# A second hand-written order for the steps of an interleaved convolution loop

## The chip, the cores and the metric

One Trainium2 chip, one of its cores. The metric is the device time of one launch in microseconds (us), the median of several runs. Engines are named as in the profile: PE (TensorE, matmuls), DVE (VectorE), ACT (ScalarE), POOL (GpSimd), SP (the queue that issues most DMAs). In this kernel POOL's instructions read and write SBUF alone; those of DVE and ACT also read PSUM.

## What is computed

A block with two halves. The first normalizes x (2048 x 640), modulates it, and applies a state-space convolution along the 2048 positions; the second is a gated feed-forward layer. What matters here is the first half, above all its kernel K:

```python
dt = jnp.exp(log_dt)[:, None]
logdA = dt * (A_re + 1j * A_im)                # 640 channels x 128 states
P = jnp.exp(logdA[:, :, None] * l)             # l = 0 .. 2047
K = jnp.einsum("dn,dnl,dn->dl", Cc, P, dt * Bc).real
y = irfft(rfft(u, 2 * L) * rfft(K, 2 * L))[:, :L] + u * Dskip
x = x + ga * y                                 # u is the normalized, modulated x
h = layernorm(x) * (1 + cb) + sb
x = x + gb * ((silu(h @ w1) * (h @ w3)) @ w2)
```

## The kernel before

The kernel runs in three stretches: tables, modulation and a first transform of x (to about 168 us), the convolution (to about 420 us), and the feed-forward layer (the rest, bound by PE's matmuls). The change lies in the convolution.

The 640 channels are cut into NS = 40 steps of SD = 16 channels. For each step k, two pipelines of named parts are run, one that makes the kernel's transform for the 16 channels, one that multiplies and inverts transforms made earlier (its index runs ten ahead of its own first block: its step k works on the block (k - 10) // 8 of 128 channels, part (k - 10) % 8).

Making the kernel, step k:

- `PH` (`phases`, POOL): two integer instructions, L469 over 1024 and L470 over 512 elements, give the angles `ph`. There are four `ph` buffers: PH of k waits until both readers on DVE of k - 4, `A1` and `A2`, are through.
- `AB`, `CO`, `SI` (`absph`, `cosine`, `sine`, ACT): the absolute value, then cosine and sine of the angles, into `cs` (three buffers) and back into `ph`.
- `PA`, `XA`, `PQ`, `XQ` (`exp_fast`, `fast`, `exp_slow`, `slow`): two small matmuls on PE into a PSUM tile, ACT's exponential out of it into the table `A`; then the same with another matmul pair. All four use one PSUM buffer, tag "B", so that they run strictly one after the other over all steps.
- `E1`, `E2`, `A1`, `A2` (`real1`, `real2`, `imag1`, `imag2`, DVE; L494, L497, L501, L505): products of `A` with cosine and sine. Both inputs and the output are in SBUF.
- `kg` (`kgen`, PE, L518): 64 small matmuls into the PSUM tile `pk` (one buffer).
- `K` (`k1evac`, DVE, L525 and L526): reads `pk` from PSUM.
- `pt` (`k_stage1`, PE, L536), `uk` (`k_out`, ACT): first stage of the transform of K.

The convolution, step k:

- `st` (`stage2`, PE, L567): second stage of both transforms into the PSUM tile `p` (one buffer: st of k waits for Y of k - 1).
- `kc` (`k_copy`, ACT): half of `p` to SBUF.
- `T` (`products`, DVE, L584 and L585) and `Y` (`sums`, DVE, L591 and L592): the complex product; each of these four instructions has one input in PSUM.
- `iv` (`inverse1`, PE, L609) into the PSUM tile `pz` (one buffer for two steps), `zt` (`z_store`, ACT and DMA): the inverse transform out to DRAM.

Loads (`s2` in stage2, `i1` in inverse1, `uk` from DRAM in `u_load`) and the stores of `zt` are issued on SP.

The order in which these parts stand on each engine is written out by hand in the list `ROUND` (L823). It is a list of words such as `XA+4`; round `rnd` runs `XA` of step 4 * rnd + 4, and skips what is out of range or already done. One round holds four steps of each part (two stores `zt`). `in_order[0] = True` before the loop makes `keep` hold every engine's instructions in the order in which the list names them. The steps up to about 10 are done before the loop, in another order, and the last of the convolution (from step 42 on) after it. Instructions of different engines are tied only by their data and buffers; the list sets no order between engines.

ACT has to load a table when it goes between the exponentials (`XA`, `XQ`) and the cosine and sine.

## Time and profile before

| what | us |
|---|---|
| median of 3 runs | 987.19 |
| the runs | 982.88, 987.19, 990.32 |
| the profiled execution | 988.51 |
| its span in the trace | 986.7 |

The trace is that of the profiled execution. Its times start at the span's start. In the trace the convolution's first `T` starts at 168.69 us and its last at 415.35; `PH` of the last step starts at 351.24 us. Lines with an "x" and a count are groups; durations are in ns in views by tile or by line and in us in the timeline. A bracket at the end of a timeline row gives the idle time of that engine ahead of the instruction and what the profile holds to have ended it. "PEclk" is the clock granted to PE as a share of the full one.

### The profile page before, as it was taken

How to read it: one execution, taken by the hardware profiler on the slowest of the kernel's cores; microseconds unless marked ns; L12 is line 12 of the kernel's file. 1: busy time of each engine (PE TensorE's matmuls, PEld its weight loads, DVE VectorE, ACT ScalarE, POOL GpSimd, SP SyncE). 2: the span in 40 equal slices, each digit the busy share in tenths (PEclk: the TensorE clock that was granted, in tenths of full speed). 3: DMA queues.
4: the chain of work that ended last, by engine and by line, in shares of the span. 5: the costliest groups of instructions: out<-in, count | busy, mean ns of one | idle time of the engine just before them, and what ended most of it. 6: DMA issues, size and time to landing. Idle time of an engine off the chain costs nothing.

```text
span 986.7 us, 20165 instructions
## 1 busy us (share of the span) xinstructions
PE 897.5 (91%) x7984; PEld 675.2 (68%) x7984; DVE 719.0 (73%) x1259; ACT 545.4 (55%) x797; POOL 275.3 (28%) x278
## 2 busy tenths in 40 slices
PE   4896787888788889889999999999999999999998
PEld 2443444666666666567788888777888888888886
DVE  5598876999999997667766665568796766654575
ACT  4568675989999884246533332355653333323432
POOL 1473233455454550213522220112152222200000
PEclk8657787999999999989999999999999999999999
DMA  9462576544655477767211311897422221112443
GB/s 264 154 239 103 204 195 195 154 124 142 169 156 145 147 210 217 246 179 250 81 45 59 107 57 54 213 270 225 135 93 67 81 67 54 54 41 87 153 147 121
DMA packets 103570, 140.72 MB, mean 143 GB/s; under 512 B 20564, under 2 KB 62676, under 8 KB 103476
## 3 DMA queue, kind: packets, MB, share of 16 engines
q1 hardware_dynamic: 99668, 129.34, 43.9%
q0 software_dynamic: 2304, 7.74, 2.3%
q10 hardware_dynamic: 1504, 2.36, 0.8%
q8 instruction: 63, 1.03, 0.4%
q14 instruction: 31, 0.25, 0.1%
HBM read 107.94 MB, written 31.46 MB: 141 GB/s over the span
## 4 chain that ended last, share of the span: by engine, by line
PE 67%; DVE 17%; ACT 7%; DMA 4%; issue 3%; SPq 1%; POOL 0%; ACTq 0%; DVEq 0%; POOLq 0%
PE ps L102 54%; DVE E L494 3%; DVE E L497 3%; PE p L567 2%; PE pk L518 2%; DMA zs<-zt 2%; PE pz L609 2%; ACT cs L135 1%; PE pt L536 1%; DVE p L585 1%; DVE A L501 1%; ACT ph L135 1%; DVE T L584 1%; DVE A L505 1%; PE pu L408 1%
## 5 line engine op out<-in xcount | busy, mean ns | idle before, releaser
L102 DVE TENSOR_TENSOR s<-ps,s 128x512 f32<-128x512 f32 x138 | 94.9, 688 | 79.9 <-PE ps L102 79.6
L469 POOL TENSOR_TENSOR ph<-thi,iota 128x1024 int32<-128x1024 int32 x40 | 85.5, 2137 | 166.2 <-DVE pk L525 61.6
L102 DVE TENSOR_TENSOR gl<-rw,gh 128x640 fp32r<-128x640 f32 x87 | 78.2, 899 | 67.5 <-ACT gh L102 67.4
L102 ACT CAST gh<-rw 128x640 fp32r<-128x640 f32 x87 | 63.3, 727 | 106.3 <-PE ps L102 62.5
L567 PE MATMUL p<-uk,s 128*64 128x256 f32 x640 | 79.7, 391 | 14.5 <-issue 9.0
L102 PE MATMUL ps<-xA,gh 128*128 128x512 f32 x280 | 87.9, 392 | 0.4 <-ACT xA L102 0.4
L102 PE MATMUL ps<-gh,uh 128*128 128x512 f32 x224 | 87.4, 390 | 0.0
L102 PE MATMUL ps<-gl,uh 128*128 128x512 f32 x224 | 87.2, 389 | 0.0
L102 POOL TENSOR_TENSOR S<-rw 128x256 f32<-128x256 f32 x46 | 36.7, 800 | 173.9 <-DVE S0l L102 154.8
L102 PE MATMUL ps<-gh,ul 128*128 128x512 f32 x208 | 81.1, 390 | 0.0
L567 PEld LDWEIGHTS p<-uk,s 128*64 128x64 f32 x640 | 46.2, 140 | 38.6 <-issue 14.1
L102 PEld LDWEIGHTS ps<-xA,gh 128*128 128x128 f32 x280 | 52.1, 188 | 13.0 <-ACT xA L102 1.0
L494 DVE TENSOR_TENSOR E<-A,cs 128x1024 f32<-128x1024 f32 x40 | 56.1, 1402 | 5.9 <-ACT cs L135 5.2
L518 PE MATMUL pk<-E 128*32 128x64 f32 x1280 | 46.5, 235 | 14.1 <-DVE K L526 14.0
L102 PE MATMUL ps<-xA,gl 128*128 128x512 f32 x140 | 54.5, 390 | 0.0
L518 PEld LDWEIGHTS pk<-E 128*32 128x32 f32 x1280 | 32.9, 117 | 30.5 <-DVE K L526 17.3
L470 POOL TENSOR_TENSOR ph<-ph,phi 128x512 int32<-128x512 int32 x40 | 51.7, 1292 | 4.0 <-DVE phi L293 1.0
L536 PE MATMUL pt<-s,K 128*64 128x128 f32 x640 | 49.1, 295 | 1.8 <-ACT uk L138 1.8
L609 PE MATMUL pz<-Y,i 64*128 64x128 f32 x640 | 46.1, 285 | 4.0 <-ACT zt L138 3.7
L501 DVE TENSOR_TENSOR A<-A,ph 128x1024 f32<-128x1024 f32 x40 | 49.1, 1227 | 0.0
L609 PEld LDWEIGHTS pz<-Y,i 64*128 64x128 f32 x640 | 40.3, 191 | 12.3 <-issue 6.0
L102 ACT ACTIVATE s<-ps 128x512 f32<-128x512 f32 (+1 forms) x33 | 19.7, 597 | 51.5 <-PE ps L102 51.5
(255 smaller groups left out, 2291.8 us busy)
## 6 DMA issues: line engine op xcount, KB each, us to landing
rw<-in_w_dram SPq DMA_DIRECT2D x52, 320.0 KB
us<-u SPq DMA_DIRECT2D x16, 640.0 KB
s<-in_s_dram SPq DMA_DIRECT2D x40, 256.0 KB
i<-in_i_dram SPq DMA_DIRECT2D x40, 256.0 KB
rw<-in_wg_dram SPq DMA_DIRECT2D x31, 320.0 KB
rw<-in_wu_dram SPq DMA_DIRECT2D x28, 320.0 KB
uk<-us SPq DMA_DIRECT2D x32, 256.0 KB
zs<-zt SPq DMA_DIRECT2D x32, 256.0 KB
```

The costliest lines, as they stand in the source:

```text
L102: ins = fn(*args, **kw)
L135: return tc.keep_in_program_order(S.activation(*args, **kw))
L408: PE.matmul(pu[h][hh * 64:hh * 64 + 64, q, :320], s1r[r], x[r, hh * 320:hh * 320 + 320], start=not (one and h == 0), stop=True, tile_posit ...
L469: hold(G.tensor_tensor(p, bc(thi[:, sl], 2, NPH), bc(iota, 1, SD), op=OP.mult))
L470: keep(G.tensor_tensor(p[:, :, :NA], p[:, :, :NA], bc(phi[:, sl], 2, NA), op=OP.add))
L494: keep(V.tensor_tensor(EC[s][:, :, 1:3, :], AA[s][:, :, 1:3, :], mid(cs[s]), op=OP.mult))
L497: keep(V.tensor_tensor(EC[s][:, :, 0, :], AA[s][:, :, 0, :], cs[s][:, :, 2 * NA - 1:NA - 1:-1], op=OP.mult))
L501: keep(V.tensor_tensor(A[:, :, 1:3, :], A[:, :, 1:3, :], mid(ph[s]), op=OP.mult))
L518: keep(PE.matmul(pk[dq * 32:dq * 32 + 32, g, :], x[:, g * 4 + dq, 1, :], x[:, g * 4 + dq, 0:3:2, :], start=(st == 0), stop=(st == 1), tile ...
L536: keep(PE.matmul(pt[c * 64:c * 64 + 64, g, :], kk[:, g, :], s1[:, c, :], start=True, stop=True, tile_position=(0, c * 64)))
L567: keep(PE.matmul(p2[par * 64:par * 64 + 64, pi, c, :], s2[:, pi * 2 + par, c * 64:c * 64 + 64], uk[:, 0:kn + 1:kn, f, :], start=True, stop ...
L609: ins = keep(PE.matmul(pz[:, par, (g % 2) * 2 + pi, :], i1[r, pi, c, :], Y[r, pi, c, :], start=(c == 0), stop=(c == 1), tile_position=(par ...
```

## The change

Only the list `ROUND` is replaced. Both lists hold the same 22 parts, `zt` for two steps and each other part for four, so the work of a round is the same; what differs is the order, and how far apart the steps of different parts stand. No instruction, buffer or DMA is added or taken away.

```diff
     ROUND = (
-        "A1+0 pt-2 K-1 st+1 CO+1 E1+1 iv-1 uk-2 pt-1 kc+1 zt-1 kg+0 PH+4 T+1 CO+2 uk-1 E2+1 Y+1 SI+1 E1+2 "
-        "st+2 A2+1 K+0 AB+4 SI+2 E2+2 SI+4 CO+3 A1+1 kc+2 A2+2 CO+4 PA+4 iv+0 pt+0 SI+3 kg+1 T+2 iv+1 Y+2 "
-        "E1+3 XA+4 A1+2 st+3 PQ+4 kc+3 XQ+4 PA+5 uk+0 K+1 XA+5 zt+1 kg+2 T+3 PQ+5 PH+5 XQ+5 pt+1 PA+6 Y+3 "
-        "AB+5 XA+6 E2+3 st+4 PH+6 AB+6 A1+3 PQ+6 A2+3 XQ+6 kc+4 iv+2 uk+1 PA+7 E1+4 E2+4 PH+7 K+2 XA+7 T+4 "
-        "kg+3 AB+7 A2+4 PQ+7 Y+4 XQ+7 "
+        "XA+6 PQ+6 pt+2 A2+3 AB+6 XQ+6 kc+4 A1+4 PH+7 T+4 uk+2 PA+7 iv+2 Y+4 kg+3 K+3 XA+7 CO+5 A2+4 PQ+7 "
+        "st+5 AB+7 kg+4 kc+5 E1+5 T+5 CO+6 iv+3 SI+7 SI+5 K+4 Y+5 pt+3 PH+8 uk+3 E2+5 E1+6 A2+5 A1+5 st+6 "
+        "zt+3 AB+8 E2+6 SI+6 kc+6 iv+4 CO+7 T+6 CO+8 iv+5 kg+5 SI+8 XQ+7 pt+4 Y+6 K+5 st+7 PA+8 PH+9 uk+4 "
+        "A2+6 XA+8 PQ+8 kc+7 XQ+8 A1+6 E1+7 kg+6 PH+10 AB+9 T+7 PA+9 pt+5 Y+7 K+6 XA+9 E1+8 uk+5 PQ+9 E2+7 "
+        "XQ+9 E2+8 zt+5 A1+7 PA+10 st+8 "
     ).split()
     in_order[0] = True
     for rnd in range(NS // EB + 3):
```

On DVE a round reads before: A1 K E1 T E2 Y E1 A2 K E2 A1 A2 T Y E1 A1 K T Y E2 A1 A2 E1 E2 K T A2 Y. It reads after: A2 A1 T Y K A2 E1 T K Y E2 E1 A2 A1 E2 T Y K A2 A1 E1 T Y K E1 E2 E2 A1.

## The prediction, on record before the changed kernel ran

> **What bounds the kernel now.** The change touches only the convolution, so I went first to the busy time by windows, cut where the product `T` of every fourth step begins; between 182.50 and 355.00 lie six rounds (first, second and last two rows of the seven; the last is the drain behind the final `PH`).

> ```profile
> core 0: us, PE busy (x) PEld busy (x) DVE busy (x) ACT busy (x) POOL busy (x), PEclk, DMA share, GB/s
> 182.50:211.10 28.60, 23.41 (x472) 17.55 (x472) 27.73 (x41) 26.51 (x33) 14.15 (x9) 1.00 0.55 153
> 211.10:240.00 28.90, 24.81 (x472) 18.93 (x472) 26.28 (x41) 26.47 (x32) 14.36 (x9) 0.94 0.48 135
> ...
> 326.00:355.00 29.00, 24.85 (x472) 18.55 (x472) 27.19 (x42) 26.57 (x32) 16.69 (x13) 0.94 0.57 159
> 355.00:384.00 29.00, 26.29 (x578) 20.47 (x580) 25.94 (x47) 16.85 (x23) 5.26 (x9) 1.00 0.67 190
> ```

> A round lasts (355.0 - 182.5) / 6 = 28.75 us. DVE is busy for up to 27.73 of it, ACT for 26.5, PE for 23.4: DVE is first, but ACT is only 1.2 us behind. That sets how far the time can fall. Next, by tile, the durations of the instructions concerned (min/median/max):

> ```profile
> L469 POOL TENSOR_TENSOR ph<-thi,iota x40: 1892/1906/2819, 15.7 to 351.2; 128x1024 int32<-128x1024 int32 x40
> L470 POOL TENSOR_TENSOR ph<-ph,phi x40: 1042/1047/2109, 18.6 to 354.1; 128x512 int32<-128x512 int32 x40
> L494 DVE TENSOR_TENSOR E<-A,cs x40: 1160/1219/2670, 49.0 to 370.3; 128x1024 f32<-128x1024 f32 x40
> L497 DVE TENSOR_TENSOR E<-A,cs x40: 634/683/2389, 51.1 to 375.3; 128x512 f32<-128x512 f32 x40
> L501 DVE TENSOR_TENSOR A<-A,ph x40: 1209/1218/1494, 53.6 to 375.9; 128x1024 f32<-128x1024 f32 x40
> L505 DVE SCALAR_TENSOR_TENSOR A<-ph,A x40: 677/683/693, 55.2 to 377.0; 128x512 f32<-128x512 f32 x40
> L584 DVE TENSOR_TENSOR T<-p,kc x40: 676/681/693, 168.7 to 415.3; 128x512 f32<-128x512 f32 x40
> L585 DVE TENSOR_TENSOR p<-p,kc x40: 699/699/700, 169.4 to 416.1; 128x512 f32<-128x512 f32 x40
> L591 DVE TENSOR_TENSOR Y<-T,p x40: 411/420/422, 170.2 to 416.8; 128x256 f32<-128x256 f32 x40
> L592 DVE TENSOR_TENSOR Y<-T,p x40: 412/415/421, 170.5 to 417.1; 128x256 f32<-128x256 f32 x40
> L525 DVE TENSOR_TENSOR pk<-pk,dz x40: 155/163/171, 70.3 to 380.3; 128x4 f32<-128x4 f32 x40
> L526 DVE TENSOR_TENSOR K<-pk,gaT x40: 401/424/427, 71.1 to 380.5; 128x256 f32<-128x256 f32 x40
> ```

> The six DVE instructions that read PSUM never stray by more than 26 ns from their least, whatever else runs. E1 and E2, all in SBUF, sometimes take 2.2 and 3.5 times their median, and so do the two of PH. The timeline shows why (rows of other instructions left out):

> ```profile
> 259.33 1.90 POOL L469 TENSOR_TENSOR ph<-thi,iota 128x1024 int32<-128x1024 int32 x1 [2.36 <-DVE pk L525]
> 259.65 0.68 DVE L584 TENSOR_TENSOR T<-p,kc 128x512 f32<-128x512 f32 x1
> 260.05 1.02 ACT L135 ACTIVATE A<-pa 128x1024 f32<-128x1024 f32 x1
> 260.36 0.70 DVE L585 TENSOR_TENSOR p<-p,kc 128x512 f32<-128x512 f32 x1
> 261.31 1.05 POOL L470 TENSOR_TENSOR ph<-ph,phi 128x512 int32<-128x512 int32 x1
> ...
> 261.86 0.61 ACT L135 ACTIVATE A<-pq 128x512 f32<-128x512 f32 x1
> ...
> 263.97 0.68 DVE L505 SCALAR_TENSOR_TENSOR A<-ph,A 128x512 f32<-128x512 f32 x1
> ...
> 264.57 1.21 DVE L494 TENSOR_TENSOR E<-A,cs 128x1024 f32<-128x1024 f32 x1
> 264.79 2.75 POOL L469 TENSOR_TENSOR ph<-thi,iota 128x1024 int32<-128x1024 int32 x1 [2.43 <-DVE A L505]
> 265.71 2.39 DVE L497 TENSOR_TENSOR E<-A,cs 128x512 f32<-128x512 f32 x1
> 267.62 1.37 POOL L470 TENSOR_TENSOR ph<-ph,phi 128x512 int32<-128x512 int32 x1
> ```

> At 259.33 PH runs beside T, and both take their medians. At 264.79 PH starts 0.14 us after A2's end, but E1 has begun; PH's first part ends at 267.54, that is, it ran its 1.9 us only from E1's end on, and E2, issued at 265.71, stood still meanwhile. So a PH instruction and a DVE instruction with both inputs in SBUF exclude each other, whole instructions at a time, and the first to start holds. What that costs is read from the groups in 195 to 350 us:

> ```profile
> L494 DVE TENSOR_TENSOR E<-A,cs 128x1024 f32<-128x1024 f32 x21 | 30.3, 1445 | 3.9 <-ACT cs L135 3.9
> L497 DVE TENSOR_TENSOR E<-A,cs 128x512 f32<-128x512 f32 x21 | 25.6, 1221 | 0.0
> ```

> 21 x ((1.445 - 1.219) + (1.221 - 0.683)) = 16.0 us in 21 steps, 0.76 a step, 3.05 us a round of DVE standing still. The chain of waits runs through it (in order of time: start, us, what):

> ```profile
> 264.65 1.14 DVE E L494
> 265.79 2.31 DVE E L497
> 268.69 1.30 PE pk L518 x64
> ```

> **The change, part by part.** Nothing is added or removed, so the sum is one of waits.

> *DVE.* PH of a step starts when its buffer is free, after A1 and A2 of four steps back. In the new list behind the later of the two stands, each time, one more SBUF instruction (A1+4, E1+5, E2+6, E1+7) and then the run T, Y, K. If that SBUF instruction starts first, PH waits for it and then runs 1.906 + 1.047 and a gap of 0.08 (261.31 less 259.33 less 1.90) = 3.03 us beside T, Y, K, whose medians add up to 0.681 + 0.699 + 0.420 + 0.415 + 0.163 + 0.424 = 2.80. The next SBUF instruction waits about 0.3 us (0.23, and some for the overlap of neighbours). Four times 0.3 is 1.2 a round in place of 3.05: 1.85 off DVE, from 27.73 to 25.9. That lets ACT's 26.5 be the bound.

> *ACT and PE.* What becomes late is the chain of the single buffer "B". From an exponential XA to its XQ the rows at 260.05 and 261.86 give 1.81 us. Between XA+8 and XQ+8 the list puts a copy (kc), between XA+9 and XQ+9 another (uk): XA and one copy fill about 1.5 us, so ACT waits about 0.3 twice. Between PA+10 and the following PQ+6 PE has the whole of st+8:

> ```profile
> 263.00 1.95 PE L567 MATMUL p<-uk,s 128*64 128x256 f32 x16
> ```

> XQ then comes about 1.95 + 0.75 after XA (0.75 is PQ to XQ, 1.81 less XA's 1.02 and a hand-over), filled by XA and AB for 2.0: another 0.5 to 0.7. So ACT's new waits are 0.9 to 1.3 us; with its 26.5 busy, of which a few tenths are tails that a follower overlaps, the round is 27.1 to 27.8. I take 27.4: 28.75 - 27.4 = 1.35 saved, in six rounds 8.1 us.

> [...]

> *The start.* While ACT waits for the first `st`, the old list has A2 of step 10 and the sine of step 12 done; the new one names them behind kc of step 10.

> ```profile
> 168.07 0.59 ACT L138 COPY kc<-p 128x512 f32<-128x512 f32 x1 [7.84 <-PE p L567]
> L135 ACT ACTIVATE ph<-ph x40: 1037/1051/1069, 46.1 to 366.6; 128x1024 f32<-128x1024 int32 x40
> ```

> The cover of 7.84 us is gone for both: on ACT 1.05, on DVE 0.68, at the same time if neither is late otherwise. Between 0 and 1.7, I take 1.0, the larger. *The drain* (355 on) has no PH to exclude, and the two lists end on the same parts: nothing, plus or minus 1. *DMA*: the list sets no order on SP, and where its loads will fall among the stores is not to be read from this trace; nothing is taken for it, with rival (2) as the bound above.

> The sum: 8.1 - 1.0 = 7.1 us off 988.51, 981.4. That execution lies 1.3 above the median of 987.19 and inside 982.88 to 990.32, so beside that median 980, and 981 is taken between the two.

> **The rivals.** (1) *PH gets in first at one E1 a round.* E1+5 needs CO+5, and PH+8 needs A2+4; both hang on the matmul PA+7: CO+5 behind XA and a table load on ACT, A2+4 behind iv and kg on PE and K on DVE.

> ```profile
> 254.83 1.16 PE L609 MATMUL pz<-Y,i 64*128 64x128 f32 x16
> 255.68 1.28 ACT L135 ACT_TABLE_LOAD   x1
> ```
> ```profile
> L135 ACT ACTIVATE cs<-cs,hp x40: 1136/1150/1158, 45.0 to 365.1; 128x1024 f32<-128x1024 f32 x40
> ```
> ```profile
> 297.59 1.10 PE pk L518 x64
> ```

> That is 1.02 + 1.28 + 1.15 = 3.45 for E1 against 1.16 + 1.10 + 0.59 + 0.68 = 3.53, and 0.14 for POOL to start: E1 first, but by 0.2 only. If POOL wins, E1 waits 1.9 us, and T+5, whose kc is ready by then, with it; part of that is swallowed where DVE waits for ACT later in the round. [...] The round is then 28.0 to 28.5: 4.5 to 1.5 saved, less 1.0, for 984 to 987 beside that median. For it: the tie. Against: a DVE that is late for any other reason finds E1's inputs ready and goes first.

> (2) *Slower: PH first at E1+5 and at E1+7 as well.* E1+7 needs XQ+7, which the new list puts behind kc+6, two cosines, a sine and a table load: 2 x 1.15 + 1.05 + 1.28 + 0.61 = 5.24 us, while A1+6, on which PH+10 waits, ends 2.80 + 0.68 + 1.22 = 4.70 behind kc+6 if DVE is not late. If it is less than about 0.4 us late, POOL wins here. DVE then stands 2 x 1.9 more and is spared 0.3 twice: 25.9 + 3.2 = 29.1, plus what it idles now, 28.6 - 27.73 = 0.9: 30.0 a round. That is 1.25 x 6 + 1.0 = 8.5 lost: 996. Against: a loss at one of the two makes DVE late, and so wins the other.

> (3) *All the gain.* ACT's waits vanish behind one another: 26.5, 2.25 x 6 - 1.0 = 12.5 saved, 975. PH and the SBUF instructions, which exclude each other, take 4 x (3.03 + 1.219 + 0.683 + 1.218 + 0.683) = 27.3 by medians, and 26.2 if each of 16 overlaps its follower by the 0.07 us of E1 at 264.57; less is not to be had, and 973 is the floor.

> **How the numbers follow.** Chances: the forecast 0.45, rival (1) 0.20, rival (2) 0.15, rival (3) 0.20. The forecast alone, 27.1 to 27.8 with its start and drain, is 976 to 984; rivals (1) and (3) widen it to 973 and 987, and the drain and the spread of the runs to 990; rival (2) is left out. A difference under 1%, 9.9 us, is taken as none. Faster by more needs 977.3 or less: most of rival (3) and a quarter of the forecast, 0.28. Slower by more needs 997.1: most of what rival (2) holds, with a late load on SP as another way there, 0.15. The rest, 0.57, is neither.

> **What would show it.** Right: the window of a round at 27 to 27.8; the means of E1 and E2 at 1.3 and 0.8 us or less; PH at its medians with T, p, Y and pk beside it; ACT at 95% with waits on PE at XQ. Wrong: rows of E1 over 2 us (rivals 1 and 2), or PE waiting for loads of `s2` and `i1`.

## The result, and the profile after

| what | before | after |
|---|---|---|
| median of 7 runs, us | 983.54 | 975.61 |
| the runs, us | 982.79 to 990.62 | 971.78 to 978.43 |
| the profiled execution, us | 988.51 | 975.61 |
| its span, us | 986.7 | 973.8 |

The ratio of after to before is 0.989, that of the means of the seven runs (985.8 and 975.0 us), with a 95% interval of 0.9854 to 0.9927: 1.1% faster, about 10.8 us, between 7 and 14. The medians lie 7.9 us apart. The forecast was 981 us with "no change over 1%" as the likeliest outcome; the time lies within the range of 973 to 990, and the gain lies above the forecast 7.1. By the means the change is just over 1%, with 1% still inside the interval.

The busy time by windows, cut as before where the product `T` of steps 12, 16, 20 and so on begins (the first two of six rounds, the last, and the drain from T of step 36 to that of 42 and of 49):

```profile
181.13:208.50 27.37, 23.47 (x474) 17.55 (x472) 26.01 (x41) 26.54 (x33) 14.75 (x9) 1.00 0.58 151
208.50:235.87 27.37, 23.47 (x474) 17.55 (x472) 26.03 (x42) 26.52 (x33) 14.75 (x9) 1.00 0.59 155
...
317.98:345.67 27.69, 23.78 (x480) 17.83 (x478) 26.34 (x42) 26.85 (x34) 17.31 (x13) 1.00 0.68 177
...
345.67:378.53 32.86, 30.44 (x624) 23.13 (x624) 26.22 (x49) 20.86 (x30) 8.21 (x11) 1.00 0.86 222
378.53:402.19 23.66, 22.60 (x264) 14.94 (x260) 17.81 (x41) 8.53 (x14) 2.44 (x4) 1.00 0.94 296
```

A round takes 27.37 us, five times within 0.01. ACT is busy for 26.5 of it, 97%, where it was 92%. DVE went from 27.7 to 26.0 busy and is no longer first. No round is granted less than the full PE clock; before, three of six were at 0.94.

The groups of E1 and E2 in 195 to 345 us of the kernel after (count, then busy us in all and mean ns of one, then the idle time before them):

```profile
L494 DVE TENSOR_TENSOR E<-A,cs 128x1024 f32<-128x1024 f32 x22 | 35.2, 1598 | 1.4 <-ACT cs L135 1.4
L497 DVE TENSOR_TENSOR E<-A,cs 128x512 f32<-128x512 f32 x22 | 14.6, 685 | 0.0
```

E2, 1221 ns in the mean before, is at its median: that collision is gone. E1 has become worse, 1598 ns against 1445. The timeline of the kernel after shows one E1 a round that PH gets ahead of:

```profile
238.50 1.15 ACT L135 ACTIVATE cs<-cs,hp 128x1024 f32<-128x1024 f32 x1
238.60 0.79 DVE L505 SCALAR_TENSOR_TENSOR A<-ph,A 128x512 f32<-128x512 f32 x1
239.53 1.90 POOL L469 TENSOR_TENSOR ph<-thi,iota 128x1024 int32<-128x1024 int32 x1 [0.69 <-DVE A L505]
...
239.68 2.84 DVE L494 TENSOR_TENSOR E<-A,cs 128x1024 f32<-128x1024 f32 x1 [0.29 <-ACT cs L135]
...
242.44 0.68 DVE L584 TENSOR_TENSOR T<-p,kc 128x512 f32<-128x512 f32 x1
```

A2+4 ends at 239.39, PH+8 starts 0.14 us later, and the cosine that E1+5 needs ends at 239.65: POOL wins by 0.15 us. E1 then lasts 2.84 instead of 1.22. This is the event of rival (1); its price was not the one given there.

Three traces of each list split the gain: the ones above, the repeats b_ctl and a_ctl, and d_before and d_after, which hold back four loads within the drain and are otherwise the same kernels. Each figure is the difference of two starts of `T`, in us, and the traces stand in that order:

| stretch | old list | new list | means, new less old |
|---|---|---|---|
| T of step 10 to step 12 | 13.84, 13.85, 13.84 | 14.14, 14.15, 14.15 | +0.3 |
| step 12 to 36, six rounds | 172.47, 172.06, 172.05 | 164.54, 164.49, 164.51 | -7.7 |
| step 36 to 49, the drain | 60.35, 59.04, 61.26 | 56.52, 56.63, 57.00 | -3.5 |

They add up to -10.9 us, about the gain of the ratio; without the d pair the drain is -3.1. What lies ahead of step 10 is not touched by the list and moved by itself between 164.7 and 170.0 us; from step 49 to the end of the span it is 571.3 to 571.6 us in all four traces of the two kernels themselves.

### The profile page after: what moved, and what is told of

It reads as the page before. It is cut to its first block, busy times and chain, and to the rows that moved or that the text cites. A ratio compares the mean times of both kernels' runs of the same rounds, so it can differ in the third digit from the quotient of the medians.

```text
span 973.8 us, 20146 instructions
## 1 busy us (share of the span) xinstructions
PE 895.1 (92%) x7984; PEld 672.5 (69%) x7984; DVE 711.6 (73%) x1259; ACT 546.5 (56%) x798; POOL 279.3 (29%) x278
## 3 DMA queue, kind: packets, MB, share of 16 engines
q1 hardware_dynamic: 99668, 129.34, 46.1%
q10 hardware_dynamic: 1504, 2.36, 0.7%
## 4 chain that ended last, share of the span: by engine, by line
PE 76%; ACT 10%; DVE 6%; DMA 4%; issue 3%; POOL 1%; ACTq 0%; SPq 0%; POOLq 0%; DVEq 0%
PE ps L102 55%; PE p L567 6%; ACT A L135 3%; PE pk L518 3%; PE pz L609 3%; PE pt L536 2%; ACT cs L135 2%; DMA zs<-zt 2%; PE pq L441 1%; PE pm L301 1%; PE pa L431 1%; PE pu L408 1%; ACT uk L138 1%; DMA uk<-in_w_mod_dram 1%; ACT L135 1%
## 5 line engine op out<-in xcount | busy, mean ns | idle before, releaser
L469 POOL TENSOR_TENSOR ph<-thi,iota 128x1024 int32<-128x1024 int32 x40 | 91.9, 2297 | 153.9 <-DVE A L501 54.6
L567 PE MATMUL p<-uk,s 128*64 128x256 f32 x640 | 79.4, 390 | 13.9 <-ACT uk L138 5.8
L567 PEld LDWEIGHTS p<-uk,s 128*64 128x64 f32 x640 | 45.9, 139 | 37.8 <-issue 10.1
L494 DVE TENSOR_TENSOR E<-A,cs 128x1024 f32<-128x1024 f32 x40 | 60.4, 1510 | 2.9 <-ACT cs L135 2.2
L470 POOL TENSOR_TENSOR ph<-ph,phi 128x512 int32<-128x512 int32 x40 | 49.5, 1239 | 4.0 <-DVE phi L293 1.0
L501 DVE TENSOR_TENSOR A<-A,ph 128x1024 f32<-128x1024 f32 x40 | 49.9, 1247 | 0.0
L102 PEld LDWEIGHTS ps<-gl,uh 128*128 128x128 f32 x224 | 42.1, 188 | 9.0
L102 PEld LDWEIGHTS ps<-gh,uh 128*128 128x128 f32 x224 | 42.1, 188 | 8.7
L518 PE MATMUL pk<-E 128*32 128x64 f32 x1280 | 46.2, 233 | 1.9 <-issue 1.1
L536 PE MATMUL pt<-s,K 128*64 128x128 f32 x640 | 46.0, 283 | 1.8 <-ACT uk L138 1.8
L609 PE MATMUL pz<-Y,i 64*128 64x128 f32 x640 | 44.5, 283 | 3.0 <-ACT zt L138 2.3
L609 PEld LDWEIGHTS pz<-Y,i 64*128 64x128 f32 x640 | 39.4, 189 | 10.9 <-ACT zt L138 5.2
```

Source lines behind the costliest of these rows:

```text
L102: ins = fn(*args, **kw)
L469: hold(G.tensor_tensor(p, bc(thi[:, sl], 2, NPH), bc(iota, 1, SD), op=OP.mult))
L470: keep(G.tensor_tensor(p[:, :, :NA], p[:, :, :NA], bc(phi[:, sl], 2, NA), op=OP.add))
L494: keep(V.tensor_tensor(EC[s][:, :, 1:3, :], AA[s][:, :, 1:3, :], mid(cs[s]), op=OP.mult))
L501: keep(V.tensor_tensor(A[:, :, 1:3, :], A[:, :, 1:3, :], mid(ph[s]), op=OP.mult))
L518: keep(PE.matmul(pk[dq * 32:dq * 32 + 32, g, :], x[:, g * 4 + dq, 1, :], x[:, g * 4 + dq, 0:3:2, :], start=(st == 0), stop=(st == 1), tile ...
```

## Experiments

**What makes the old round long, and what bounds the new one.** Two kernels cut PH, two cut the cosine. PH of steps 13 on was cut in both lists to one of 16 channels:

```diff
 ...
+        n = SD if s < 13 else 1
-        hold(G.tensor_tensor(p, bc(thi[:, sl], 2, NPH), bc(iota, 1, SD), op=OP.mult))
+        hold(G.tensor_tensor(p[:, :n], bc(thi[:, sl], 2, NPH)[:, :n], bc(iota, 1, SD)[:, :n], op=OP.mult))
 ...
```

The second instruction and the buffer that is kept are left out here.

> The old list, with PH of steps 13 on cut to one of 16 channels (the other angles stay as an earlier step left them), so that POOL hardly occupies SBUF. Exclusion as the cause: E1 and E2 fall to their medians (1.22 and 0.69 us in the mean), DVE loses its 3.05 us of standing still, and the round falls from 28.75 to 26.5 to 27.4 us, where ACT's 26.5 us bind. The rival, that the old order of PE's and ACT's work made the round long and the new list mended that: the round stays at 28.2 us or more.

> The new list with the same small PH. If ACT binds the new round (26.53 us busy of 27.37), it stays at 26.9 to 27.4 us, although the one E1 a round that takes 2.84 us falls to 1.22. If that lost E1 (1.6 us) is on the path, the round falls to 25.8 to 26.3 us.

The old list's windows with the small PH, the first two of six, and then the new list's, first two:

```profile
183.35:209.93 26.58, 23.33 (x478) 17.55 (x477) 24.29 (x41) 26.19 (x33) 3.61 (x8) 1.00 0.61 161
209.93:236.50 26.57, 23.34 (x478) 17.54 (x476) 24.29 (x40) 26.18 (x33) 3.62 (x8) 1.00 0.57 155
```
```profile
180.47:208.64 28.17, 24.89 (x474) 18.72 (x472) 24.55 (x41) 26.29 (x33) 5.74 (x10) 0.94 0.57 145
208.64:235.61 26.97, 23.44 (x474) 17.27 (x474) 24.56 (x40) 26.55 (x33) 4.81 (x7) 1.00 0.60 158
```

E1 and E2 come to 1.22 and 0.71 us in the mean, and the old order falls by 2.0 us a round at full clock (28.53 to 26.57), to 98% ACT. So PH is what made the round long, and the old order of ACT's and PE's work is no worse than the new, rather 0.3 to 0.4 better (26.57 against 26.84 to 26.97 at full clock). The new list loses 0.4 to 0.5 us a round to PH in all, though its E1 stands for 1.6: ACT binds. Two of its six rounds were granted 0.94 and took 28.17, 1.2 us more, which neither expectation allowed for.

One thing this run doesn't separate. A PH that E1 holds up is also late for ACT, which waits for it in every round of the kernel before (182.5 to 355 us: 4.7 in all, 6 times, 1.1 at most):

```profile
ACT cs L135 <- POOL ph L470: 4.7, 6, 1.1
```

The small PH takes away this wait together with DVE's standing still.

The cosine of steps 13 on was cut to half of its channels:

```diff
-        act(cs[s], cs[s], AF.Sin, scale=-2 * math.pi / TURN, bias=hp)
+        c = cs[s] if s < 13 else cs[s][:, :SD // 2]
+        act(c, c, AF.Sin, scale=-2 * math.pi / TURN, bias=hp)
```

> The new list, with the cosine of steps 13 on over half of its channels (the other half keeps the absolute value of the angle), 0.55 us less on ACT a step, 2.2 a round. If ACT binds, the round falls from 27.37 to where DVE stands: 26.0 to 26.4 us. If DVE or PE binds, it stays at 27.2 to 27.4 us.

> The old list, with the cosine of steps 13 on over half of its channels (the other half keeps the absolute value of the angle): 2.2 us less on ACT a round. If DVE, with what it stands still for PH, binds the old round, it stays at 28.2 to 28.8 us, against a fall of 1.5 us that the same cut gave under the new list. If ACT's work binds the old round as well, it falls by 1 us or more.

New list, then old list, two rounds each:

```profile
180.71:206.60 25.89, 23.48 (x474) 17.55 (x472) 24.41 (x42) 24.96 (x33) 14.74 (x9) 1.00 0.62 158
206.60:232.48 25.88, 23.29 (x474) 17.35 (x472) 24.41 (x41) 24.94 (x33) 14.74 (x9) 1.00 0.61 164
```
```profile
212.04:240.57 28.53, 24.76 (x472) 18.82 (x472) 27.50 (x41) 24.87 (x32) 14.15 (x9) 0.94 0.50 141
240.57:269.11 28.54, 23.42 (x472) 17.56 (x472) 28.09 (x42) 24.89 (x32) 14.16 (x9) 1.00 0.55 151
```

With less work on ACT the new round falls by 1.48 us and the old one, at full clock, not at all: ACT's work binds the new round and not the old one, where DVE is busy for 28.09 of 28.54. Less ACT work also settled the tie: E1 came to 1.23 us in the mean under the new list, and DVE no longer waits for its cosine there.

**The ties.** a_swap puts A2+4 behind E1+5 in the new list; a_both also puts A1+6 behind E1+7 (the second pair of lines below is a_both's alone; quotes and line ends of the list are left out).

```diff
-XA+7 CO+5 A2+4 PQ+7 st+5 AB+7 kg+4 kc+5 E1+5 T+5
+XA+7 CO+5 PQ+7 st+5 AB+7 kc+5 E1+5 A2+4 kg+4 T+5
 ...
-PQ+8 kc+7 XQ+8 A1+6 E1+7 kg+6 PH+10 AB+9 T+7 PA+9 pt+5
+PQ+8 kc+7 XQ+8 E1+7 A1+6 PH+10 AB+9 T+7 PA+9 kg+6 pt+5
```

> The new list with A2+4 put behind E1+5 (and kg+4 behind it), so that PH+8 starts only when E1+5 is through. E1 falls from a mean of 1.64 us to 1.22. If E1's lost 1.6 us lies beside an idle DVE and reaches ACT only through the cs buffer that AB+8 waits 0.34 us for, the round falls from 27.37 to 26.9 to 27.2 us, 1 to 3 us off the kernel. If the lost E1 is on the path in full, it falls to 26.0. If K and the matmuls behind the moved kg+4 become late, it rises over 27.5.

E1+5 is spared, and the mean of E1 stays at 1.62 us all the same: DVE now comes earlier to A1+6, and PH+10 gets ahead of E1+7. From the timeline of a_swap:

```profile
237.81 1.23 DVE L494 TENSOR_TENSOR E<-A,cs 128x1024 f32<-128x1024 f32 x1 [0.34 <-ACT cs L135]
...
251.06 0.60 ACT L135 ACTIVATE A<-pq 128x512 f32<-128x512 f32 x1
251.56 1.90 POOL L469 TENSOR_TENSOR ph<-thi,iota 128x1024 int32<-128x1024 int32 x1 [1.83 <-DVE A L501]
...
251.69 2.85 DVE L494 TENSOR_TENSOR E<-A,cs 128x1024 f32<-128x1024 f32 x1 [0.28 <-ACT A L135]
```

Four of the six rounds took 27.65 to 27.68 us and the first and last 28.3 and 28.2; the kernel's ratio to before is 0.9922 (0.9892 to 0.9952). The expectation of 26.9 to 27.2 failed: it did not see that the other tie would turn.

> The new list with both ties taken out: A2+4 and kg+4 behind E1+5 as in a_swap, and A1+6 behind E1+7 with kg+6 behind PA+9. No PH can then start ahead of an E1 that waits for ACT. The mean of E1 falls from 1.64 to 1.22 us. If the lost E1 is what a round has left to gain, it falls to 26.9 to 27.1 us, as with the small PH. If the moved matmuls hold up the exponentials, it stays at 27.4 us or rises.

With both ties out E1's mean is 1.29 us, and the round takes 28.43 us, or 29.7 to 29.8 at 0.94 of the clock (31.0 in the first, at 0.89); ratio 1.0045 (1.0012 to 1.0078). ACT's waits in these rounds (180 to 357 us) are for `pt`, which stands behind the moved kg+6 on PE:

```profile
ACT uk L138 <- PE pt L536: 14.1, 12, 2.3
```

That is 2.4 us a round, against 0.5 in a_swap and none in the kernel after. The moved matmuls cost more than the two E1: the order on PE and ACT is worth more here than the lost 1.6 us on DVE.

**The largest collision in the old list.** o_fix moves E2+4 and A2+4 behind the instructions that read PSUM; o_fix2 moves AB+7 as well.

```diff
-PA+7 E1+4 E2+4 PH+7 K+2 XA+7 T+4 kg+3 AB+7 A2+4 PQ+7 Y+4 XQ+7
+PA+7 E1+4 PH+7 K+2 XA+7 T+4 kg+3 AB+7 PQ+7 Y+4 E2+4 A2+4 XQ+7      (o_fix)
+PA+7 E1+4 PH+7 K+2 XA+7 T+4 kg+3 PQ+7 Y+4 E2+4 A2+4 XQ+7           (o_fix2)
-A1+0 pt-2 K-1 st+1 CO+1 E1+1
+A1+0 pt-2 K-1 st+1 CO+1 AB+3 E1+1                                  (o_fix2)
```

> The old list with one pair of words moved: E2+4 and A2+4 stand behind K+2, T+4 and Y+4, so that PH+7 runs beside these. Exclusion as the cause: the E2 that took 2.39 us falls to about 1.0, the mean of E2 from 1.22 to about 0.85, and the round from 28.7 to 27.0 to 27.4 us, as far as the whole new list went. The rival, that the rest of the new order made the gain: 28.3 us or more.

E2 fell to 0.74 us in the mean, and nothing was gained: rounds of 28.6 and 29.7 us, ratio 1.0038 (1.0007 to 1.0069). ACT's waits in o_fix's rounds (177 to 350 us) say where it went:

```profile
ACT cs L135 <- DVE E L497: 9.7, 6, 1.6
ACT kc L138 <- PE p L567: 5.8, 6, 1.6
```

Six times 1.6 us: `cs` has three buffers, AB+7 waits for E2+4 to free one, and E2+4 now comes late. The mean of E2 had been the wrong thing to watch alone.

> The old list with E2+4 and A2+4 behind K+2, T+4 and Y+4 as in o_fix, and AB+7 moved behind the next round's CO+1, so that ACT no longer stands 1.61 us for the cs buffer that the later E2 frees. If the wait for that buffer is what ate the gain there, the round falls from 28.6 to 26.9 to 27.4 us. If something else in the old order binds, it stays over 28.

The wait is gone, the round falls to 27.43 to 27.51 us, ratio 0.9922 (0.9893 to 0.9951). Three words moved in the old list thus give what the whole new list gives in the rounds. But the collision isn't gone. The groups of o_fix2 in 195 to 345 us:

```profile
L494 DVE TENSOR_TENSOR E<-A,cs 128x1024 f32<-128x1024 f32 x22 | 37.5, 1704 | 0.0
L497 DVE TENSOR_TENSOR E<-A,cs 128x512 f32<-128x512 f32 x21 | 17.1, 816 | 0.0
```

Together E1 and E2 take 2.5 us in the mean, where they took 2.7 (1445 and 1221 ns): an E1 of up to 2.67 us has taken E2's place. What did go is ACT's wait for PH, of which there is none in these rounds, nor in those of the kernel after. So the gain doesn't follow DVE's standing still alone: a_both, with 0.5 us a round of it left, has rounds of 28.43 us. How much of the old round was DVE's loss and how much the late PH, no run here separates.

**The drain.** b_ctl and a_ctl are the two kernels once more.

> The kernel before once more, for a second trace of it. If the 3.5 us that the stretch from the T of step 42 to that of step 49 gained (27.2 us before, 23.7 us after) belong to the new list, this trace shows 27.2 again, give or take 0.5, and rounds of 28.75 us in the mean. If they are a matter of the run (DMA engines 99% busy there, one store that ACT waits 4.19 us for), the stretch comes out anywhere from 23 to 27 us while the rounds stay at 28.5 to 28.9 us.

> The changed kernel once more, for a second trace. Its runs lie between 971.8 and 978.4 us. If PE's clock makes that spread, some rounds here are granted 0.94 and last 28.2 to 28.6 us (the small-PH version of this list paid 1.2 us for such a round), the others 27.37. The stretch from the T of step 42 to that of step 49 comes out at 23 to 25 us if the list gained there, up to 27 if that is a matter of the run.

The rounds came out as in the first traces (28.53 to 28.97, and 27.36 to 27.68 us); the stretch from T of step 42 to that of step 49 took 24.88 us under the old list and 23.83 under the new. So part of the old list's 27.17 was the run. The new list's two traces, 975.61 and 978.32 us, differ ahead of step 10 (166.99 against 169.95 us) and not in the rounds.

h_on runs the old list for the first eight rounds and the new one from there on; h_no the reverse. FIRST and THEN are the two lists; h_no starts the second range at 8.

```diff
-    for rnd in range(NS // EB + 3):
-        for word in ROUND:
+    for rnd, words in [(r, FIRST) for r in range(8)] + [(r, THEN) for r in range(7, NS // EB + 3)]:
+        for word in words:
```

> The old list for the first eight rounds and the new one from there on, so that only the drain (from the T of step 36) is in the new order. That stretch up to the T of step 49 took 60.4 and 59.0 us under the old list and 56.5 and 56.6 under the new. If the new list's own order of the drain makes the difference, it takes 56 to 57.5 here. If it is a matter of the run or of what the rounds leave behind, 59 or more. Rounds before that: 28.5 to 28.9 us.

> The reverse: the new list for the first eight rounds, the old one for the drain. Rounds of 27.37 us up to step 32. If the order of the drain is what gains there, the stretch from the T of step 36 to that of step 49 takes 59 to 61 us; if not, 56 to 57.5.

From T of step 36 to that of 49 h_on took 56.5 us, h_no 62.8, more than the 59 to 61 expected and than any trace of the old list (59.0 to 61.3). The stretch follows the order of the drain, whichever list ran ahead of it. Windows of step 36 to 42 and 42 to 49, h_no and then the kernel before:

```profile
348.42:383.79 35.37, 30.50 (x628) 23.36 (x628) 27.25 (x48) 19.99 (x29) 8.20 (x11) 1.00 0.76 200
383.79:411.26 27.47, 23.70 (x260) 15.56 (x258) 17.80 (x40) 8.63 (x14) 2.44 (x4) 0.94 0.89 274
```
```profile
355.00:388.18 33.18, 30.38 (x626) 23.39 (x628) 27.05 (x49) 19.18 (x29) 5.79 (x10) 1.00 0.72 199
388.18:415.35 27.17, 23.80 (x260) 15.55 (x258) 17.80 (x41) 8.54 (x14) 2.43 (x4) 0.94 0.89 277
```

Two differences stand out against the changed kernel's rows above: DMA is busier in its first part (0.86 against 0.76 and 0.72) and less is left for the second, and the second part of the old drain is granted 0.94. d_before and d_after test the first, by holding back the four early loads of the next stage (the line stands twice):

```diff
-        with tc.issue_after(i1_last[0].ins):
+        with tc.issue_after(zlast[0].ins):
```

> The kernel before, with the four early loads of the feed-forward stage (two of x, two of weights, 320 KB each) held back until the last store of the convolution is issued. If the stretch from the T of step 42 to that of step 49 is long because its stores share saturated DMA engines with what has not been moved earlier (7.53 MB there, against 7.0 to 7.2 MB under the new drain), it falls from 24.9 to 27.5 us to 22 to 23.5. If the old order of the drain holds it up in another way, it stays over 24.5. The feed-forward stage starts later, so the whole time says nothing.

> The changed kernel with the same four loads held back. By the same reason its stretch falls from 23.7 to 22 to 23 us, no more than 1 us apart from that of the old drain; if loads are not the cause, it stays at 23.6 to 23.8 and the old one over 24.5.

Step 42 to 49, old list and then new:

```profile
385.59:411.85 26.26, 23.75 (x260) 15.40 (x258) 17.80 (x40) 8.53 (x14) 2.44 (x4) 0.94 0.82 239
```
```profile
377.04:400.90 23.86, 22.67 (x264) 14.93 (x260) 17.70 (x40) 8.83 (x15) 2.76 (x5) 1.00 0.80 249
```

The DMA share fell in both (to 0.82 and 0.80), the times did not. Contention with those four loads is not the reason. What the old drains share is a wait of PE in the second part, though from step 42 on both kernels run the same order, which stands behind the loop. PE's wait and then ACT's for a store, kernel before and kernel after, in that part:

```profile
PE pz L609 <- ACT zt L138: 2.1, 1, 2.1
ACT zt L138 <- DMA zs<-zt: 5.3, 2, 4.2
```
```profile
PE pz L609 <- issue: 0.7, 2, 0.4
ACT zt L138 <- DMA zs<-zt: 4.3, 5, 1.3
```

The inverse transform needs the one `pz` emptied by `zt`, and `zt` needs a buffer that an earlier store still reads. In four traces of the old drain (before, b_ctl, d_before, h_no) PE waits 2.1, 1.1, 2.1 and 2.8 us there, in four of the new one (after, a_ctl, d_after, h_on) 0.2 at most; the longest wait for a store is 3.0 to 4.2 us against 1.3 to 2.3. The lower clock comes with that wait: in the kernel before PE waits until 405.95 us, and 3.41 us at half the clock start at 405.97; the second part is granted 0.94 in d_before and h_no too, and 1.00 in b_ctl, where the wait is 1.1. The old drain is long without it too: that of b_smallph, granted 1.00 in both parts, took 26.5 us in the second, with a wait of 2.4.

Over the three traces of each list PE is busy for 55.0 us of the drain against 53.1, and idle for 5.2 against 3.6. So of the 3.5 us about 1.9 are the same work at a lower clock and 1.6 are waits. Why the stores land later under the old list was not tried.

**The parts together.** best runs o_fix2's list for eight rounds and the new list from there.

> The list of o_fix2 for the first eight rounds (27.45 us each, and 12.5 us from the T of step 10 to that of step 12 against 14.1 under the new list) and the new list's drain from there (56.5 us from step 36 to 49, against 58.3 in o_fix2). If the three parts add, it is 1 us faster than the changed kernel and 12 us faster than the kernel before, a ratio of 0.988; if the seam costs what the start gains, 0.989 to 0.992.

975.02 us in the median of 6 runs, ratio 0.9902 (0.987 to 0.9933). In its trace the first stretch takes 12.47 us, four rounds 27.44 to 27.52 and the drain 56.8, as expected, but two rounds take 28.6 and 28.8: one was granted 0.94, the other is the seam. It beats the kernel before and not the changed one.

## Why the prediction was right about the rounds and wrong about the drain

- *DVE stands 3.05 us a round for PH, and this is what the change takes away.* That PH's hold makes the old round long is shown: without it the round falls to 26.58 (b_smallph). DVE's busy time came to 26.0, forecast 25.9, but from another split: 1.8 us a round of standing still are left, 1.6 in one E1 and 0.2 in two A2 (0.79 us, as at 238.60, in place of 0.68), where 1.2 were forecast as four short waits. The prediction also left out ACT's wait for PH, 0.8 us a round before and none after.
- *ACT binds the new round, at 27.1 to 27.8, 27.4 taken.* Shown: 27.37, and less work on ACT shortens the new round (a_halfco) and not the old one (b_halfco). The six rounds gave 7.7 us; 8.1 was forecast. That the size came so near is in part luck: the waits behind the number were not the ones named. Those of ACT over the six rounds of the kernel after are:

```profile
ACT cs L135 <- DVE E L497: 2.0, 6, 0.3
ACT A L135 <- PE pa L431: 1.2, 6, 0.2
```

  0.33 a round for the `cs` buffer and 0.2 for PA; XQ, whose waits were to make 0.9 to 1.3 us a round, has under 0.1 us of idle time ahead of it each time. The prediction did not look at the three buffers of `cs` at all, and o_fix shows what they can cost.
- *Rival (1).* POOL does win at E1+5, every round. Its price was wrong: 28.0 to 28.5 was given, and the round is 27.37, since DVE now idles for 1.35 us a round that can take up part of it; the small PH puts all of PH's cost in the new list at 0.4 to 0.5 us. That losing one tie wins the other, the argument held against rival (2), holds in the kernel after, and a_swap shows the converse.
- *The clock.* The sum has no term for dips, rounds granted less than the full clock. The new rounds have none; the old ones have three, two and two in the three traces. At 0.37 us each (28.90 less 28.53) that is 0.9 in the mean of the 7.7 us, and 6.8 without them.
- *The start.* 1.0 us was taken as lost, 0.3 was.
- *The drain, "nothing, plus or minus 1".* This is the step that failed. It gave 3.5 us, a third of the gain. The reason given, that the two lists end on the same parts and no PH excludes anything there, looks at DVE, which does not bind that stretch: PE is busy for 53.0 of 56.5 us of it in the kernel after. h_on and h_no show that the list decides between 56.5 and 59 to 63 us there. What the term left out is PE's path: its waits for `pz`, behind stores, and the clock that drops with them. Why the old list brings these waits about stays open.
- *The chances.* 0.57 on no change over 1% followed from 7.1 us; 10.8 lies just over the 9.9 us that this allowed. The sum had one term set to zero for lack of a view of it, so its bound should have been wider, on the side of the gain too.

## What to carry to other kernels

Where a fixed order is exchanged, cut the windows at the same step in both kernels and forecast each stretch, the drain as well: the engine that binds the steady part need not bind the end. Before moving an instruction off a collision, list what frees its buffers: E2 moved out of PH's way cost ACT through the `cs` ring what DVE had gained, and with that mended the collision fell on an E1. Two instructions that exclude each other and become ready 0.15 us apart, as PH+8 and E1+5 do here (E1 2.84 us in place of 1.22), give the loss to one place or another; measure the loss with the excluding work cut away before spending an order on it.

## What the runs showed of the hardware

```profile
208.00:211.41 3.41, 1.29 (x28) 0.98 (x28) 3.38 (x5) 2.49 (x4) 3.33 (x2) 1.00 0.49 158
211.41:214.82 3.41, 3.41 (x78) 3.02 (x74) 3.38 (x6) 1.98 (x3) 0.16 (x1) 0.50 0.00 1
```

  Every other stretch of that grid in the convolution has PE at 50% (from 303.57) or more, and no dip behind it. In b_ctl the matmuls slow down from about 207.9, 265.9 and 351.3 us on, 17 and 25 times that length apart, with 37 to 40% ahead. Around its third wait PE is at 38% in 3.41 us from 319.0 on, but at about 48% in the stretch of the grid, from about 320.5. On the grid of the kernel after, counted back from its first dip behind the convolution (404.76), PE is never under 59% from 169 to 401 us. Near one half it goes either way: with the new list and the small PH a dip at about 199.4 has 49% ahead of it. So the same wait of 2.1 us came with a dip or without, by where it fell on the grid; what makes the grid was not tried.
